# Attention and MLP in one kernel: norms and q/k loads pair by pair in a ring of six, the MLP three units behind the attention instead of four

## The chip, the cores and the metric

The kernel runs on one core of one Trainium2 chip. Times are device microseconds (us) of one execution, as medians over several. Engines: PE (matmul), DVE (VectorE), ACT (ScalarE), POOL (GpSimd), SP (SyncE, which here only issues DMAs). DMAs issued by SP form one queue; those issued by POOL, which convert float32 to bfloat16 on the way, form another. Fast executions of one kernel differ by up to some 1.5%. Runs more than that above the fastest count as slow; they are kept out of all ratios and verdicts, but the medians and ranges quoted below are of all runs.

## The reference

```python
def _attn_ref(q, k, v, tau):                       # (8, 12, 448, 64), tau 0.1
    q_n = q / (np.linalg.norm(q, axis=-1, keepdims=True) + 1e-06)
    k_n = k / (np.linalg.norm(k, axis=-1, keepdims=True) + 1e-06)
    scores = np.matmul(q_n, k_n.transpose(0, 1, 3, 2)) / tau
    attn = np.exp(scores - np.max(scores, axis=-1, keepdims=True))
    attn = attn / (np.sum(attn, axis=-1, keepdims=True) + 1e-09)
    return np.matmul(attn, v)
def _moe_ref(x, w_in, w_out):                      # x (3584, 768), w_in (768, 2048)
    h = x @ w_in
    return (h * np.cos(h)) @ w_out
```

The heads of one batch, side by side, are the 768 columns of x for its 448 tokens.

## The kernel before

A *pair* is two heads (g, 48 of them), a *unit* three pairs (u, 16), a batch two units. For a pair, POOL squares q and k, DVE sums the squares (`reduce`), ACT makes the reciprocal norm by Ln and Exp (`rnorm`), POOL scales; PE transposes, multiplies q by k; ACT takes the exponentials; PE multiplies by v (`attend`) and also forms the sums of the softmax. Once a unit is done, its sums take a way of their own, the *chain of the sums*, before x is ready:

```python
    def gather(u):      # SP: four small DMAs, sums out of xu into 128 partitions
    def recip(u):       # DVE: add the two halves, reciprocal
    def spread(u):      # SP: DMA to scratch in DRAM
    def broadcast(u):   # SP: two DMAs, 64 copies of each row back into RB (0.69 MB written)
    def normalise(u, p, eng="DVE"):
        i, b = u % 2, u // 2
        P.op(eng, lambda e: e.tensor_tensor(xTv[b % 2][:, UP * i + p, :], xuv[i][:, 0, p, :], RBv[:, p, :], ALU.mult),
             ["RB", ("xu", i, p)], [("xT", b % 2, UP * i + p)])
```

The MLP of a batch is `m1` (W1, 96 matmuls in 8 groups, cos and product) and `m2` (W2), whose matmuls are given out in portions of 8 as fills between the attention of later pairs. What is done when stands in the loop below; `kq` counts four places in each of a unit's three pairs. In the traces each engine takes its instructions in the order in which the program names them: a copy that is ready still stands behind a normalise that waits (shown below at 325.52).

```python
    LAG = 4
    FILLS = ((8, 8, 8, 8, 8, 8, 8, 8, 8, 0, 8, 0), (8, 8, 8, 8, 16, 8, 8, 8, 8, 8, 8, 16))
    def around(u, kq):
        ...
        if kq == (4 if u == 0 else 0) and u + 2 < NU:
            load(u + 2, 0, UP)                    # q and k of a whole unit, 1.38 MB, SP
        if u + 1 < NU:
            ...                                   # x is kq (kq - 1 in unit 0)
            if 0 <= x < 3:
                squares(u + 1, x, ...)            # POOL, a unit ahead
            if 2 <= x < 5:
                reduce(u + 1, x - 2)
            if x == 5:
                rnorm(u + 1, 0, UP)
            if 6 <= x < 9:
                scale(u + 1, x - 6)               # POOL
        if kq == 1 and u >= 1 and u + 1 < NU:
            load_v(u + 1)                         # POOL's DMA queue
        if kq in (1, 4, 7):
            load_w()
        if u >= 1:
            if kq == 2:
                gather(u - 1)
            if kq == 5:
                recip(u - 1)
                spread(u - 1)
            if kq == 8:
                broadcast(u - 1)
        if u >= 2 and kq < UP:
            normalise(u - 2, kq, "POOL" if early else "DVE")
    ...
            if p == 0 and u >= LAG and u % 2 == 0:
                m1((u - LAG) // 2)
                steps = list(FILLS[((u - LAG) // 2) % 2])
```

With a lag of four, unit 2b + 1 is normalised in unit 2b + 3 and needed by `m1` of batch b in unit 2b + 4: a unit of slack.

## Time and profile before

| | before |
|---|---|
| median (3 runs) | 530.25 us (524.15 to 532.13) |
| profiled run | 528.39 us, span 526.6 us |
| first m1 starts | 103.65 us |
| from there to m1 of batch 6 | 334.5 us |
| from there to m1 of batch 7 | 42.4 us |
| from there to the end | 46.0 us |

The kernel has an opening, in which PE waits, and a dense part, in which PE is the bound. I call the time from one m1 to the next a cycle, counted from 0: six pairs, with 80 fills in the even ones and 112 in the odd ones. These are the first four cycles before, as busy time in stretches (length, then PE, PE loads, DVE, ACT, POOL with the number of instructions, granted clock, DMA share, GB/s):

```profile
103.65:158.59 54.94, 50.07 (x369) 24.79 (x370) 28.12 (x34) 37.29 (x45) 25.32 (x15) 1.00 0.41 90
158.59:216.23 57.64, 57.64 (x417) 29.36 (x418) 32.60 (x43) 40.19 (x47) 24.27 (x15) 1.00 0.55 124
216.23:271.14 54.91, 52.44 (x386) 26.23 (x384) 26.05 (x32) 34.71 (x43) 23.87 (x14) 1.00 0.43 100
271.14:330.62 59.48, 57.71 (x417) 29.36 (x418) 32.41 (x43) 40.37 (x47) 24.27 (x15) 1.00 0.56 117
```

PE needs 57.6 us for an odd cycle and 52.4 for an even one, at full clock. One broadcast in the order of time (start, duration, engine and line, what, and in brackets how long the engine stood idle for whom):

```profile
205.59 1.10 SPq L373 DMA_DIRECT2D RB<-scr  x2
207.49 0.34 SPq L250 DMA_DIRECT2D raw<-in_q_dram  x1
...
210.97 0.68 DVE L380 TENSOR_TENSOR xT<-xu,RB 128x448 bf16<-128x448 f32 x1 [2.87 <-DMA RB<-scr]
211.11 0.81 POOL L257 DMA_DIRECT2D va<-in_v_dram  x1
```

The broadcast has the DMA engines to itself at first: the next q/k load is issued behind it, and v comes when it has landed. And these are the page's DMA issues (count, size of one, median us to landing):

```profile
RB<-scr SPq DMA_DIRECT2D x32, 336.0 KB, 4.7
...
va<-in_v_dram POOLq DMA_DIRECT2D x16, 336.0 KB, 7.2
```

### The profile page before, as it was taken

What the parts mean: (1) busy time and instruction counts of PE and PEld (TensorE: products, weight loads), DVE (VectorE), ACT (ScalarE), POOL (GpSimd) and SP (SyncE); (2) the same over time, 40 slices, a digit from 0 to 9 for tenths busy, and PEclk for the clock granted to TensorE, in tenths of its full rate; (3) what the DMA queues carried; (4) which work ended last, traced back from release to release, by engine and by line L of the source; (5) the groups of instructions that cost most, each with busy time, mean ns of one, the idle gap of its engine ahead of it and who ended that gap; (6) DMA issues with size and microseconds to landing.
All of it is one profiled execution on the core that took longest, in us unless ns stands there. A gap on an engine that the chain in (4) does not pass through costs nothing.

```text
span 526.6 us, 7760 instructions
## 1 busy us (share of the span) xinstructions
PE 465.4 (88%) x3241; PEld 231.1 (44%) x3247; DVE 246.6 (47%) x310; ACT 291.4 (55%) x348; POOL 195.1 (37%) x128
## 2 busy tenths in 40 slices
PE   7676272898989999999999998999899999799996
PEld 2232121353435554554445544554355544355563
DVE  5544333465527535544655453545565333512421
ACT  2666271657766668557764777367765764301400
POOL 4784656902680186207550547008530400000000
PEclk9788877799999999999999999999999999989999
DMA  8997999710765157603790296415730320222023
GB/s 202 192 214 138 210 194 184 183 22 2 179 151 103 31 139 177 148 1 92 156 211 7 67 190 151 84 31 132 148 49 12 104 68 20 54 60 61 1 61 89
DMA packets 50562, 56.85 MB, mean 108 GB/s; under 512 B 9824, under 2 KB 44128, under 8 KB 50528
## 3 DMA queue, kind: packets, MB, share of 16 engines
q1 hardware_dynamic: 36544, 44.57, 34.3%
q0 software_dynamic: 13984, 11.80, 15.0%
q8 instruction: 25, 0.41, 0.3%
q14 instruction: 9, 0.07, 0.0%
HBM read 56.62 MB, written 11.18 MB: 129 GB/s over the span
## 4 chain that ended last, share of the span: by engine, by line
PE 67%; DMA 8%; DVE 7%; ACT 6%; POOL 6%; issue 4%; SPq 2%; ACTq 0%; POOLq 0%; DVEq 0%
PE SC L390 17%; PE PO L429 17%; PE AV L390 10%; PE SC L323 5%; PE AV L334 5%; DMA sums<-xu 4%; PE SC L429 4%; ACT PX L326 4%; PE AV L340 3%; POOL qks L301 3%; PE TP L314 2%; DMA RB<-scr 2%; DVE n L282 2%; PE AV L429 2%; SPq L354 1%
## 5 line engine op out<-in xcount | busy, mean ns | idle before, releaser
L326 ACT ACTIVATE PX<-SC 112x896 bf16<-112x896 f32 x192 | 163.9, 915 | 65.3 <-PE SC L323 65.0
L301 POOL TENSOR_TENSOR qks<-raw,rn 112x1024 bf16<-112x1024 f32 (+1 forms) x47 | 87.9, 1895 | 189.8 <-ACT rn L294 189.4
L429 PE MATMUL PO<-W,gT 128*128 128x384 bf16 x704 | 128.7, 330 | 8.1 <-DVE osb L437 8.1
L323 PE MATMUL SC<-qkT 64*112 64x448 bf16 x384 | 64.6, 393 | 41.0 <-ACT PX L326 38.5
L429 PEld LDWEIGHTS PO<-W,gT 128*128 128x128 bf16 x704 | 64.0, 98 | 70.1 <-issue 17.8
L390 PE MATMUL SC<-xT,W 128*128 128x448 bf16 x480 | 94.7, 352 | 0.0
L275 POOL TENSOR_TENSOR sq<-raw 112x1024 bf16<-112x1024 f32 x43 | 81.5, 1907 | 6.7 <-DMA raw<-in_k_dram 6.5
L393 ACT ACTIVATE cosb<-SC,cst 128x896 f32<-128x896 f32 x40 | 40.3, 1008 | 49.0 <-PE SC L390 46.3
L390 PEld LDWEIGHTS SC<-xT,W 128*128 128x128 bf16 x480 | 47.0, 98 | 43.8
L282 DVE TENSOR_REDUCE n<-sq 112x16 f32<-112x1024 bf16 (+1 forms) x49 | 57.6, 1187 | 17.6 <-POOL sq L275 16.9
L395 DVE TENSOR_TENSOR gT<-SC,cosb 128x896 bf16<-128x896 f32 x40 | 43.6, 1091 | 41.7 <-ACT cosb L393 41.7
L390 PE MATMUL AV<-xT,W 128*128 128x448 bf16 x288 | 58.4, 353 | 1.1 <-ACT xu L344 1.0
L393 ACT ACTIVATE cosb<-AV,cst 128x896 f32<-128x896 f32 x24 | 24.2, 1008 | 53.4 <-PE AV L390 52.1
L323 PEld LDWEIGHTS SC<-qkT 64*112 64x112 bf16 x384 | 20.7, 127 | 72.3 <-ACT PX L326 54.5
L317 DVE COPY qkT<-TP 128x896 bf16<-128x896 bf16 x48 | 29.7, 620 | 45.9 <-PE TP L314 45.5
L380 DVE TENSOR_TENSOR xT<-xu,RB 128x448 bf16<-128x448 f32 x42 | 33.9, 816 | 32.4 <-DMA RB<-scr 32.4
L334 PE MATMUL AV<-PX,va 112*64 112x448 bf16 x384 | 48.7, 378 | 0.0
L437 DVE COPY osb<-PO 128x384 f32<-128x384 f32 x44 | 24.3, 551 | 41.8 <-PE PO L429 41.6
L390 PEld LDWEIGHTS AV<-xT,W 128*128 128x128 bf16 x288 | 27.8, 98 | 28.2 <-issue 1.5
L395 DVE TENSOR_TENSOR gT<-AV,cosb 128x896 bf16<-128x896 f32 x24 | 26.1, 1089 | 27.8 <-ACT cosb L393 27.8
L344 ACT ACTIVATE xu<-AV 128x896 f32<-128x896 f32 x37 | 34.0, 918 | 2.8 <-PE AV L340 2.8
L314 PE MATMUL TP<-ident,qks 112*128 112x112 bf16 x384 | 28.4, 218 | 3.4 <-DVE qks L301 2.6
(37 smaller groups left out, 249.5 us busy)
## 6 DMA issues: line engine op xcount, KB each, us to landing
RB<-scr SPq DMA_DIRECT2D x32, 336.0 KB, 4.7
raw<-in_q_dram SPq DMA_DIRECT2D x15, 672.0 KB, 8.1
raw<-in_k_dram SPq DMA_DIRECT2D x15, 672.0 KB, 10.0
va<-in_v_dram POOLq DMA_DIRECT2D x16, 336.0 KB, 7.2
W<-in_moe_w_in_dram POOLq DMA_DIRECT2D x6, 512.0 KB, 7.4
W<-in_moe_w_out_dram POOLq DMA_DIRECT2D x4, 768.0 KB, 7.8
out_dram<-osb SPq DMA_DIRECT2D x8, 336.0 KB, 2.7
out_dram<-osb SPq DMA_DIRECT2D x8, 288.0 KB, 2.6
```

The lines of the kernel that those rows point to most:

```text
L275: P.op(eng, lambda e, s0=s0, s1=s1: e.tensor_tensor(y[:, :, s0:s1, :], x[:, :, s0:s1, :], x[:, :, s0:s1, :], ALU.mult), [("raw", i, p, h) ...
L282: P.op("DVE", lambda e: e.tensor_reduce(out=n2[i].ap().rearrange("p (h s) -> p h s", s=NS)[:, 2 * p : 2 * p + 2, s0:s1], in_=sq[p].ap().re ...
L301: P.op(eng, lambda e, s0=s0, s1=s1: e.tensor_tensor(qksv[i][:, s0:s1, hs, :].rearrange("p s h d -> p h s d"), rawv[i][:, hs, s0:s1, :], ba ...
L314: P.op("PE", lambda e, s=s: e.transpose(TP.ap()[:, NP * s : NP * s + NP], qksv[i][:, s, 2 * p : 2 * p + 2, :], ident.ap()), [("qks", i, p, ...
L323: P.op("PE", lambda e, r=r, a=a: e.matmul(SCv[z][0:NP, a, 0:S], qkT[j].ap()[r, S + NP * c : S + NP * c + NP], qkT[j].ap()[r, 0:S], start=T ...
L326: P.op("ACT", lambda e: e.activation(PXv[j][:, c], SCv[z][0:NP, :, 0:S], ACT.Exp, scale=1.0 / TAU), ["SC%d" % z], [("PX", j, c)])
L334: P.op("PE", lambda e, a=a, c=c: e.matmul(AVv[64 * a : 64 * a + 64, 0, 0:S], vav[i][:, NJ * (2 * p + a) + c, :], PXv[j][:, c, a, :], start ...
L344: P.op("ACT", lambda e: e.activation(xuv[i][:, :, p, :], AVv[:, :, 0:S], ACT.Copy, bias=0.0), ["AV"], [("xu", i, p)])
L390: P.op("PE", lambda e, n=n, c=c, a=a: e.matmul(ph[:, a, 0:S], W1v[:, c, 128 * n : 128 * n + 128], xTv[b % 2][:, c, :], start=(c == 0), sto ...
L393: P.op("ACT", lambda e: e.activation(cosv[cz], ph[:, :, 0:S], ACT.Sin, bias=cst.ap()[:, 0:1], scale=1.0), [name, "cst"], [("cos", cz)])
L395: P.op("DVE", lambda e: e.tensor_tensor(gTv[:, 2 * gi : 2 * gi + 2, S * (b % 2) : S * (b % 2) + S], ph[:, :, 0:S], cosv[cz], ALU.mult), [n ...
L429: P.op("PE", lambda e, po=po, f=f, col=col, hf=hf: e.matmul(po[:, 0:HW], gTv[:, f, col : col + 128], W2v[:, f, HW * hf : HW * hf + HW], st ...
```

## The change

It is meant to shorten the opening: q/k are loaded, squared and scaled pair by pair in a ring of six slots, not unit by unit, so that POOL's normalise no longer holds up a whole unit and the small gathers no longer stand behind 1.38 MB; the MLP starts a unit earlier (lag 3); W1 comes in four column quarters, so that its first groups can start with a part of it. Early normalises move from POOL to DVE. The v load moves from the first to the second pair of a unit. The core, cut:

```diff
-    w_loads = [(("W1", c), ... W1v[:, c, :], moe_w_in[128 * c : 128 * c + 128, :])) for c in range(NKC)]
+    w_loads = [(("W1", x), ... W1v[:, :, WQ * x : WQ * x + WQ], moe_w_in[:, WQ * x : WQ * x + WQ] ...)) for x in range(NQ)]
...
-    LAG = 4
+    LAG = 3
+    EARLY = UP * LAG + 1
+    W_AT = {2: 1, 4: 1, 5: 1, 7: 1, 8: 1, 9: 3}
...
-    def around(u, kq):
-        ... (as shown above)
+    def around(g, at):
+        u, kq = g // UP, 4 * (g % UP) + at
+        if at == 0:
+            if g + 2 < NG:
+                rnorm(g + 2)
+                scale(g + 2)
+                if g + 2 + RR - 1 < NG:
+                    load(g + 2 + RR - 1)          # one pair, 0.46 MB
+            if g + 3 < NG:
+                squares(g + 3)
+        if at == 1:
+            for _ in range(W_AT.get(g, 0)):
+                load_w()
+            if g % UP == 1 and u + 1 < NU:
+                load_v(u + 1)
         if u >= 1:
             if kq == 2:
                 gather(u - 1)
...
             if kq == 8:
                 broadcast(u - 1)
         if u >= 2 and kq < UP:
-            normalise(u - 2, kq, "POOL" if early else "DVE")
+            normalise(u - 2, kq)
...
-            if p == 0 and u >= LAG and u % 2 == 0:
-                m1((u - LAG) // 2)
+        if g >= UP * LAG and (g - UP * LAG) % (2 * UP) == 0:
+            b = (g - UP * LAG) // (2 * UP)
+            m1(b)
```

At the end, m1 of batch 6 no longer stands behind the last pair; there are five halves of m2 instead.

## The prediction

> **What bounds the kernel now.** I read the busy time by stage first, then the chain of waits in the slow stage, then the order of time there, and last the DMA. The MLP of one batch (first matmul W1, here m1; second W2, here m2) is interleaved with the attention of later pairs of heads; g counts the 48 pairs. Busy time in stretches, us:
>
> ```profile
> 20.00:40.00 20.00, 15.60 (x124) 6.14 (x124) 10.80 (x12) 11.60 (x15) 14.24 (x11) 0.82 1.03 224
> ...
> 60.00:80.00 20.00, 10.15 (x77) 4.01 (x80) 8.58 (x11) 10.71 (x15) 12.53 (x10) 0.74 1.09 186
> 80.00:100.00 20.00, 8.28 (x63) 3.24 (x60) 6.32 (x9) 5.57 (x9) 16.59 (x12) 0.66 0.86 168
> 100.00:120.00 20.00, 19.49 (x119) 9.81 (x120) 13.56 (x12) 12.39 (x14) 4.05 (x3) 1.00 0.35 78
> ...
> 180.00:240.00 60.00, 60.00 (x440) 30.44 (x441) 30.61 (x40) 39.97 (x48) 24.04 (x14) 1.00 0.47 111
> ```
>
> Columns: length, PE, PE loads, DVE, ACT, POOL, clock, DMA share, GB/s. There are two kernels in one. Until 103.65 us, where m1 of batch 0 starts, PE is half idle and DMA is at 0.84 to 1.09. After that PE is the bound (60 of 60 us). So only the opening and the end have something to give. The chain of waits in the opening:
>
> ```profile
> 47.92 8.80 issue
> ...
> 56.76 1.13 POOL xT L380
> 57.88 1.85 POOL sq L275
> ...
> 72.72 9.73 issue
> ...
> 82.49 1.13 POOL xT L380
> 83.62 1.85 POOL sq L275
> ```
>
> Both long "issue" pieces are POOL standing in front of its normalise (xT) until the broadcast of the softmax sums (RB) has landed; squares and scaling of a whole unit (3 pairs) are queued behind it, and behind those everything: exps, scores. One unit takes 82.49 - 56.76 = 25.7 us, 8.6 us a pair, though a pair costs PE about 3.1 us when dense. The hops of that chain come from the order of time and the issues:
>
> ```profile
> 34.86 2.49 SPq L354 DMA_DIRECT2D sums<-xu  x4
> ...
> 44.72 0.76 DVE L362 TENSOR_TENSOR rcp<-sums 128x21 f32<-128x21 f32 x1 [3.24 <-DMA sums<-xu]
> ```
>
> The gather of the sums lands 7.4 us after its last issue, because 1.38 MB of q/k were put into the same queue at 32.23 us. At the end of the kernel, with no load ahead of it, the same gather takes:
>
> ```profile
> DMA to landing us min/median/max: 1.9/2.0/2.0
> ```
>
> **What the Trainium skill says.** "DMA: Bandwidth & Descriptors", section "Queues, rings and completion order": a queue's descriptors are consumed in ring order, and each DMA engine goes round the queues packet by packet. The 7.4 against 2.0 us agrees: a small transfer waits for what stands before it in its own queue, and shares with the other. "Perfetto Trace Analysis", section "Optimization Strategy": with several regimes whose limit differs, interleaving them helps; this is what a shorter lag does. "TensorE: Matmul & The Clock Gate", section "HAM oscillation": idle gaps beyond about 3.4 us drop the PE clock. The trace agrees: after a 9 us gap eight AV matmuls took 1.71 us at 68.40 instead of 0.95 at 49.95. "Perfetto Trace Analysis", section "Matmuls", asks for rotating PSUM banks; m2 with one bank pays for that at the new end, see below.
>
> **The change, part by part.**
> *DMA before m1(0).* The page gives the queues' cost: hardware 44.57 MB for 34.3% of 16 x 526.6 us, that is 247 GB/s when all engines serve it, and the casting POOL queue 11.80 MB (as written) for 15.0%, 149 GB/s. So one pair of q/k (0.459 MB) costs 1.9 us, a v load 2.3, a broadcast 2.8, all weights (6.29 MB) 42 us. Before: 6 units of q/k 33, weights 42, five v 11.5, three broadcasts 8.4, small ones about 6, sum 101 us, which is the opening's 103. After, m1(0) sits at pair 9, not 12, and needs W1 only: up to 16 pairs 30, W1 21, one W2 part 5, four v 9, two broadcasts and gathers 10, sum 75 us, of which some 5 to 8 us may come later. The other three W2 parts (16 us) fall beside m1(0), which takes 18.2 us at a DMA share of 0.35. So DMA alone would allow m1(0) at 67 to 75.
> *A new loop.* Per pair the norms now run squares, reduce, Ln and Exp, scale, and POOL may start the next pair's squares only after this scale: 1.89 (squares) + 0.04 + 1.21 (reduce) + 0.66 (reduce's end at 12.46 to scale's start at 13.12, 16 columns) + 1.88 (scale) = 5.7 us a pair. It is not free of cost, but far below 8.6.
> *The sums' chain.* The first squares follow the old start; pair 1 is scaled on POOL until 14.7, squares(2) to 16.6, reduce(2) to 17.9. With 5.7 a pair reduce(5) ends at 35.0, and the copy xu(2), late in pair 3, at 36.7. Gather 2.4 issue + 3 land (no large load ahead of it, W1 beside it), reciprocal 1.1, spread 2.5, broadcast issue and landing 7 (behind one pair's load and a W1 part): RB at about 53. DVE then does two normalises, a qkT copy and xu(5) (3.8 us) before the second gather at 57. The same chain again, 15.5 us, to 72.5, and 4.7 us for three normalises with two copies between: m1(0) at 77. The order on the engines shows that normalise(1) and m1(0) now lie in the same pair, with none between, so this chain and not DMA sets it; with the landings of the old opening (20 us a chain) it would be 86. I take 79: 24.7 us earlier.
> *The dense part.* From m1(0) to m1(6) are six cycles of six pairs. Before they took 54.9, 57.6, 54.9, 59.5, 54.7 us (starts of L390's AV groups in the chain). PE's own sum: m1 18.2 + 16 m2 matmuls 2.6 + six pairs of 3.1 + 80 or 112 fills of 0.163. For the fuller cycles that is 57.6, and they stay there, 58.2. In the others the last two pairs have 8 fills only and would run at ACT's or the loop's 5.0 to 5.7; I keep 54.5, a bit less than 54.9, since the gather no longer queues behind 1.38 MB and DVE waits less at the reciprocal (PE lost 1.24 us there at 150.49). Three of each: 338 us.
> *The end.* m1(6) and its m2 20.9. Pairs 46 and 47 have no fills: ACT sets them at 4 exps of 0.84 + one 0.92 + gaps = 4.7 each, and attend(47) 1.5: 10.9. Then five m2 halves on one bank, 2.6 + 0.75 for the evacuation in between, 16.2; beside them the last sums' chain: 2.4 + 2.0 + 0.6 + 1.9 + 4.7 + 0.6 = 12.2 plus the copy 0.9, hidden. The old end had m1(6) there, and a 3.08 us PE wait before 460.90. From m1(7) on nothing changes: 526.6 - 480.7 = 45.9.
> Sum: 79 + 338 + 20.9 + 10.9 + 16.2 + 45.9 = 510.9 us of span; the profiled run timed 528.4 for a span of 526.6, so 513 us. A check by difference: -24.7 in the opening, +9.3 for three pairs of PE work that move into the dense part, +3.2 for two pairs without fills, +3.0 for bank waits, -4.1 for waits of the old end, and some -2.5 in the cycles: -15.8, the same.
>
> **The rivals.**
> 1. The sums' chain stays at its old length (20 us or more a unit), since five weight parts still load in the opening beside it. For it: spread and broadcast took 10.9 us from 45.83 to 56.72, with the gather not concerned. Then m1(0) is at 86 to 88 and the time 520 to 522, within 2%.
> 2. The norm loop becomes the bound of the dense part. 5.7 us a loop against 5.72 us of a dense pair leaves nothing; DVE ops under POOL's load stretch (normalise 0.62 up to 2.78 us at 364.95). 0.3 us on 30 pairs is +9 us: 522. Against it: Ln/Exp has 0.65 us of slack on ACT before the third exp, and each m1 lets the loop catch up.
> 3. DMA holds m1(0) or the first m2: W1 parts are now 1 KB pieces per row and chunk instead of 4 KB, and three W2 parts go out late. A late W2 is a PE stall after m1(0), some 5 us. Against it: 18 us of m1 cover it.
> 4. Better than thought: chains without queueing, warm PE, DVE waits gone from all cycles: m1(0) at 74, cycles of 54 and 57.6: 503.
>
> **Range and chances.** My sum is 513; rivals 1 to 3 each take away 5 to 9 us and rarely come together, rival 4 gives 8 to 10. So 504 to 523. The limit of 2% against about 529 is 518.5, above my figure by a bit less than one deviation (some 7 us): faster 0.72, within 2% 0.26, slower 0.02, as no part adds more than the opening gives back.
>
> **What would show it.** The first L379 matmul (m1) at 75 to 85 us instead of 103.65; early pairs 5.7 to 6 us apart; gathers landing in 2 to 4 us, not 6.2 in the middle; POOL's 189 us of idle before scale broken into short pieces; cycles of 54 to 58 us; no PE gap over 2 us after m1(0). Wrong if m1(0) comes after 88, if PE waits in the dense part for exps behind Ln/Exp (loop), or for W2 after m1(0).

## The result, and the profile after

| | before | after |
|---|---|---|
| median, same rounds (4 runs each) | 530.83 us (524.15 to 532.13) | 553.47 us (552.81 to 555.55) |
| profiled run: span, clock | 526.6 us, 0.96 | 551.0 us, 0.95 |
| first m1 starts | 103.65 | 81.62 |
| to m1 of batch 6 | 334.5 (35 pairs) | 374.75 (36 pairs) |
| to m1 of batch 7 | 42.4 | 47.1 |
| to the end | 46.0 | 47.5 |

The ratio is 1.0477 (95% interval 1.0375 to 1.058): slower, where 513 us had been predicted. A ratio here is always the mean time of one kernel's fast runs over that of the other's in the same rounds, so not quite the ratio of the medians quoted. The kernel is correct.

The opening came out near the prediction. The sums of squares of pairs 2 to 4 in the order of time, and the first m1:

```profile
16.43 1.22 DVE L280 TENSOR_REDUCE n<-sq 112x16 f32<-112x1024 bf16 x1 [2.78 <-POOL sq L275]
...
22.09 1.22 DVE L280 TENSOR_REDUCE n<-sq 112x16 f32<-112x1024 bf16 x1 [3.92 <-POOL sq L275]
...
27.77 1.22 DVE L280 TENSOR_REDUCE n<-sq 112x16 f32<-112x1024 bf16 x1 [1.81 <-POOL sq L275]
...
81.62 4.64 PE L379 MATMUL AV<-xT,W 128*128 128x448 bf16 x12 [7.91 <-DVE xu L336]
```

The pairs are 5.67 us apart, and m1 starts 22 us earlier. But then the cycles, which the prediction had at 54.5 and 58.2:

```profile
81.62:139.19 57.57, 52.46 (x368) 25.35 (x369) 27.70 (x31) 36.21 (x50) 21.34 (x13) 0.95 0.65 136
139.19:206.16 66.97, 59.70 (x418) 29.58 (x417) 34.06 (x42) 41.82 (x55) 27.95 (x16) 0.97 0.45 105
206.16:261.31 55.15, 52.43 (x386) 26.21 (x384) 27.96 (x32) 36.22 (x50) 21.30 (x13) 1.00 0.42 102
261.31:331.99 70.68, 61.63 (x418) 30.08 (x417) 34.74 (x42) 41.82 (x55) 27.49 (x16) 0.93 0.43 100
331.99:387.44 55.45, 52.73 (x385) 26.31 (x383) 27.87 (x32) 36.22 (x50) 21.30 (x13) 0.99 0.43 102
387.44:456.37 68.93, 62.22 (x418) 30.32 (x417) 34.54 (x42) 41.82 (x55) 25.64 (x15) 0.93 0.31 69
```

The odd cycles take 67 to 71 us, for the same matmuls (417 or 418) that took 57.64 before, and at a lower clock, so that PE is even "busier". DMA is not full on average (0.31 to 0.45 in the odd cycles). What PE waited for from 81.62 to 456.37 (total us, times, longest):

```profile
PE AV L379 <- DVE xT L369: 12.5, 7, 3.4
PE PO L418 <- DVE osb L426: 12.5, 9, 3.9
...
PE SC L312 <- DVE qkT L306: 2.5, 3, 0.8
```

Before, in its dense part, the osb wait was 5.0 us and the other two were not there. (osb is the copy that frees the one PSUM bank of m2; xT is the normalised input of m1.) All three come from DVE, which is busy for half the time only. PE waits for no v in these cycles, though v lands late too (9.2 us). In total DVE does not stand longer in front of RB than before (30.1 us in these cycles, 31.7 before); what differs is when it gets on: 8.0 to 10.8 us after the broadcast's issue, against 5.2 to 6.6. Why DVE is late, at the start of m1 of batch 1, in the order of time:

```profile
130.81 0.44 SPq L252 DMA_DIRECT2D raw<-in_q_dram  x1
130.88 0.81 POOL L258 DMA_DIRECT2D va<-in_v_dram  x1
...
131.29 0.48 SPq L252 DMA_DIRECT2D raw<-in_k_dram  x1
131.81 1.11 SPq L362 DMA_DIRECT2D RB<-scr  x2
...
142.24 0.62 DVE L369 TENSOR_TENSOR xT<-xu,RB 128x448 bf16<-128x448 f32 x1 [4.38 <-DMA RB<-scr]
...
142.93 0.36 PE L379 MATMUL AV<-xT,W 128*128 128x448 bf16 x1 [2.99 <-DVE xT L369]
```

A pair's q and k, a unit's v and the broadcast go out within one microsecond, and the normalise comes 10.4 us after the broadcast's issue, against 5.4 in the piece shown of before. At the end of an odd cycle the same wait goes through the copies that stand behind the normalise on DVE:

```profile
325.52 1.96 DVE L369 TENSOR_TENSOR xT<-xu,RB 128x448 bf16<-128x448 f32 x1 [2.97 <-DMA RB<-scr]
...
327.41 0.54 DVE L426 COPY osb<-PO 128x384 f32<-128x384 f32 x1
...
328.01 4.19 PE L418 MATMUL PO<-W,gT 128*128 128x384 bf16 x16 [3.93 <-DVE osb L426]
```

Sixteen matmuls that take 2.77 us warm then take 4.19, since PE has lost its clock (0.65 from 328 to 332 us). The limit of 3.4 us that the prediction named is no sharp one here: sixteen took 4.41 after a wait of 2.08 us (at 452.13) and 2.77 after one of 2.16 (at 203.56). The first normalise here also takes 1.96 us for 0.62 alone, beside POOL's squares (325.11 to 327.00); more on that below. On the page's list of DMA issues the whole is seen in two lines:

```profile
RB<-scr SPq DMA_DIRECT2D x32, 336.0 KB, 7.5
va<-in_v_dram POOLq DMA_DIRECT2D x16, 336.0 KB, 9.2
```

Against the 338 us predicted, the dense part is 36.8 us too long. Waits of PE that before did not have make 12.5 + (12.5 - 5.0) + 2.5 = 22.5. PE busy is 341.2 us, against 3 x 57.6 + 3 x 52.4 = 330 at the clock of before: 11 us of slower matmuls. The other 3 us are waits that before had too: 5.0 for osb, 3.7 for exps and 2.4 for gT, 11.1 in all, where the prediction had left 338 - 330 = 8. So nothing is unassigned: 341.2 busy and 33.6 of waits are the 374.8.

### The profile page after: what moved, and what is told of

Its sections match the earlier page's. It is cut to its first block, busy times and chain, and to the rows that moved or that the text cites. A ratio compares the mean times of both kernels' runs of the same rounds, so it can differ in the third digit from the quotient of the medians.

```text
span 551.0 us, 7956 instructions
## 1 busy us (share of the span) xinstructions
PE 476.6 (86%) x3238; PEld 231.3 (42%) x3243; DVE 259.3 (47%) x314; ACT 304.2 (55%) x408; POOL 198.0 (36%) x124
## 4 chain that ended last, share of the span: by engine, by line
issue 47%; POOL 21%; PE 21%; DMA 6%; DVE 3%; ACT 1%; SPq 1%; POOLq 0%; DVEq 0%
POOL sq L275 14%; PE SC L379 6%; PE PO L418 6%; DMA RB<-scr 4%; POOL qks L293 4%; PE AV L379 4%; PE SC L418 2%; POOL va L258 2%; DVE osb L426 1%; PE AV L418 1%; DMA raw<-in_k_dram 1%; ACT PX L315 1%; DVE xT L369 1%; DMA scr<-rcp 1%; POOL W L437 1%
## 5 line engine op out<-in xcount | busy, mean ns | idle before, releaser
L418 PE MATMUL PO<-W,gT 128*128 128x384 bf16 x784 | 144.1, 332 | 15.2 <-DVE osb L426 15.2
L418 PEld LDWEIGHTS PO<-W,gT 128*128 128x128 bf16 x784 | 71.8, 99 | 85.0 <-DVE osb L426 22.5
L379 PE MATMUL SC<-xT,W 128*128 128x448 bf16 x480 | 96.9, 358 | 0.0
L275 POOL TENSOR_TENSOR sq<-raw 112x1024 bf16<-112x1024 f32 x47 | 91.8, 1952 | 6.4 <-DMA raw<-in_k_dram 6.4
L379 PE MATMUL AV<-xT,W 128*128 128x448 bf16 x288 | 67.6, 382 | 21.5 <-DVE xT L369 13.6
L379 PEld LDWEIGHTS SC<-xT,W 128*128 128x128 bf16 x480 | 47.8, 100 | 46.4 <-issue 4.4
L369 DVE TENSOR_TENSOR xT<-xu,RB 128x448 bf16<-128x448 f32 x48 | 43.6, 935 | 38.3 <-DMA RB<-scr 38.3
L379 PEld LDWEIGHTS AV<-xT,W 128*128 128x128 bf16 x288 | 29.0, 103 | 55.2 <-DVE xT L369 18.1
L426 DVE COPY osb<-PO 128x384 f32<-128x384 f32 x49 | 27.0, 551 | 46.0 <-PE PO L418 45.8
L312 PEld LDWEIGHTS SC<-qkT 64*112 64x112 bf16 x384 | 20.7, 127 | 57.6 <-ACT PX L315 34.3
L333 ACT ACTIVATE xu<-AV 128x896 f32<-128x896 f32 x39 | 35.8, 918 | 2.0 <-PE AV L329 2.0
## 6 DMA issues: line engine op xcount, KB each, us to landing
W<-in_moe_w_in_dram POOLq DMA_DIRECT2D x4, 768.0 KB, 11.3
```

The costliest lines, as they stand in the source:

```text
L275: P.op(eng, lambda e: e.tensor_tensor(o, x, x, ALU.mult), rd, wr)
L312: P.op("PE", lambda e, r=r, a=a: e.matmul(SCv[z][0:NP, a, 0:S], qkT[j].ap()[r, S + NP * c : S + NP * c + NP], qkT[j].ap()[r, 0:S], start=T ...
L333: P.op("ACT", lambda e: e.activation(xuv[i][:, :, p, :], AVv[:, :, 0:S], ACT.Copy, bias=0.0), ["AV"], [("xu", i, p)])
L379: P.op("PE", lambda e, n=n, c=c, a=a: e.matmul(ph[:, a, 0:S], W1v[:, c, 128 * n : 128 * n + 128], xTv[b % 2][:, c, :], start=(c == 0), sto ...
L418: P.op("PE", lambda e, po=po, f=f, col=col, hf=hf: e.matmul(po[:, 0:HW], gTv[:, f, col : col + 128], W2v[:, f, HW * hf : HW * hf + HW], st ...
```

## The experiments

Three theories stood at the start. **A**: with lag 3, m1 of a batch lies in the pair in which its last unit is normalised; it has no slack, and every delay goes into PE. **B**: the norm loop of 5.7 us a pair has become the bound (rival 2 of the prediction). **C**: the broadcast is late, because of its place behind a pair's load in SP's queue and the v load beside it. Later ones follow from the results. "Before" below is the kernel before in the rounds of the same batch of runs: 529.32, 528.78, 528.28, 528.24 and 530.59 us in the five batches.

### m1 a pair later (A)

```diff
-    EARLY = UP * LAG + 1
+    EARLY = UP * LAG + 2
-        if g >= UP * LAG and (g - UP * LAG) % (2 * UP) == 0:
-            b = (g - UP * LAG) // (2 * UP)
+        if g > UP * LAG and (g - 1 - UP * LAG) % (2 * UP) == 0:
+            b = (g - 1 - UP * LAG) // (2 * UP)
```

> The changed kernel, with the first MLP matmul of each batch (m1) one pair of heads later, so that one pair of work lies between the normalise that m1 needs and m1. Theory A (m1 and everything behind it waits for the late broadcast of the sums, because the shorter lag left no pair in between): the PE waits of about 7 us at m1 of batches 1, 3 and 5 go, the six cycles fall from 375 us to 345 to 355 us, and the time from 553 to 525 to 535 us. Rival B (the per-pair loop of squares, reduce, Ln/Exp and scale sets the dense part): the cycles stay at 370 or more and the time at 550 or more, since the loop is untouched. Rival C (the broadcast lands late because it queues behind the q/k load, and the DVE that stands in front of it holds up the PSUM evacuations, wherever m1 is): only half of the loss goes, 538 to 545 us.

549.3 us (547.39 to 550.13), ratio 1.039 (1.0352 to 1.0427). The waits for xT are gone and the m1 take 18.3 us again (18.3 to 20.0, against up to 25.4). But the wait of PE for osb is now 13.7 us and one for qkT has grown to 12.1. The lateness only changed its address: DVE still stands in front of RB, and what it does for PE stands behind it. A alone explains 4 of 23 us. (The edit moved v too: it goes out up to 2.9 us ahead of every second broadcast, and none within 17 us of the others, and RB lands in 6.3 us. So the 4 us are not purely A's.)

### Broadcast in front of the load, v load a pair earlier (C, both parts)

```diff
         if at == 0:
+            if u >= 1 and kq == 8:
+                broadcast(u - 1)
             if g + 2 < NG:
                 rnorm(g + 2)
...
-            if g % UP == 1 and u + 1 < NU:
-                load_v(u + 1)
+        if at == (2 if g < EARLY else 1) and (g == 1 or g >= UP and g % UP == 0) and u + 1 < NU:
+            load_v(u + 1)
...
-            if kq == 8:
-                broadcast(u - 1)
```

> The changed kernel, with the broadcast of the sums issued ahead of its pair's q/k load in the SP queue, and the load of v moved from the second pair of a unit back to the first, as in the kernel before. Theory A (no pair between normalise and m1): broadcasts land in about 5 us instead of 7.5, so the waits shrink by 2 to 3 us at each of 12 places, time 530 to 540 us, and some wait at m1 stays. Rival C (it is the place in the queue that costs): nearly all of the 37 us goes, time below 525 us. Rival B (norm loop): 550 us or more.

529.51 us (527.11 to 533.05), ratio 1.0061 (1.0032 to 1.009): 24 us come back by moving two DMAs (553.47 is from earlier rounds, in which before was within 1.6 us of its value here). RB lands in 4.8 us, v in 4.9. C is the main cause; norms, ring and loop are unchanged in this run.

### Lag 3 alone in the kernel before (a failed edit)

```diff
-    LAG = 4
+    LAG = 3
-                steps = list(FILLS[((u - LAG) // 2) % 2])
+                steps = list(FILLS[((u - LAG) // 2) % 2]) if u < NU - 1 else []
```

> The kernel before, with nothing changed but the lag of three units (and the end that belongs to it): q/k loads by units, norms by units, weights by rows. Theory A: m1 of batch 0 at 85 to 92 us (all ten weight loads still stand before it), then the same waits for the broadcast before m1, shorter as the broadcast lands in about 5 us: cycles 345 to 355 us, time 525 to 540 us. Rival C alone (queue place and not lag): cycles stay at 340 us as before, time 520 to 526 us. Rival B: the same 520 to 526 us.

The result was wrong (nan), and its 500.26 us mean nothing: I had left the test `u % 2 == 0`, so only 7 of 8 MLP batches were computed. The mended one follows below.

### The ring with the old lag

The change with `LAG = 4` and the end of the kernel before.

> The changed kernel, with the lag of four units and the end of the kernel before; ring, norms by pairs and weights by quarters stay. Theory A: m1 of batch 0 at 95 to 100 us, no wait at m1, cycles about 345 us with some DVE waits from the later broadcast, time 523 to 532 us, the same as before within 1%. Rival B (norm loop): cycles of 60 us and more as in the changed kernel, time 545 us or more. Rival C: DVE waits stay in the odd units, time 535 to 545 us.

545.3 us (541.66 to 546.06), ratio 1.0301 (1.0246 to 1.0356). There is a unit of slack before m1 again and no wait for xT, and RB lands in 7.3 us as in the change. The wait for osb is 12.2 us. So the late broadcast costs 17 us even where m1 does not need it at once (528.24 with both DMAs moved, below), by way of DVE's order.

### The order alone

Of the diff for C, only the broadcast's place; v stays in the second pair.

> The changed kernel with one thing altered: the broadcast of the sums is issued ahead of its pair's q/k load; the load of v stays at the second pair of a unit. If the q/k load in the broadcast's own queue is the cost, most of the 24 us that the pair of edits gave comes back (time 530 to 537 us, broadcasts landing in about 5 us). If the load of v from the other queue, which runs at the same time, is the cost, little comes back (545 us or more, landing 7 us).

542.69 us (540.22 to 545.82), ratio 1.0289 (1.0232 to 1.0347). RB lands in 6.0 us, with v still issued 0.1 to 0.7 us ahead of all but one broadcast of the dense part and no pair's load just in front; the normalise follows 7.2 to 8.5 us after the issue. This is 11 of the 24 us; 13 stay.

### m1 later together with the DMA order, and with normalise a pair later too

The first is the two diffs together; the second adds:

```diff
-        if u >= 2 and kq < UP:
-            normalise(u - 2, kq)
+        if u >= 2 and UP <= kq < 2 * UP:
+            normalise(u - 2, kq - UP)
```

> Both cures: broadcast ahead of the q/k load, v earlier, and m1 one pair later. With the broadcast landing in 4.7 us there are still 4 to 5 us lost at m1 of batches 1, 3 and 5 (normalises slowed beside POOL, cold PE clock behind them). If that is the missing pair between normalise and m1 (theory A as a second cause), they go and the time falls from 529 to 512 to 522 us, under both kernels. If the late landing was all, it stays at 526 to 531 us.

> As the kernel with both cures, and the three normalises of a unit also moved three places later in the program (from the first pair of the next unit into its end and the second pair), so that DVE meets a broadcast that has landed. If DVE standing in front of the broadcast still costs (osb copies and qkT copies queued behind it), 3 to 8 us more come: 507 to 518 us. If the landing in 4.7 us was early enough already, nothing changes beside the kernel with both cures.

531.09 us (527.51 to 535.5), ratio 1.0056 (1.0021 to 1.0091), and 532.03 us (526.43 to 537.96), ratio 1.0055 (1.0023 to 1.0087). The first one's profile fell in the slow state and is not compared. With slack given to m1 and DMAs in order there is still no gain over before. The second brings the normalises back into m1's own pair, so it takes the slack away again: PE waits 9.0 us for xT, and m1 of batches 1, 3 and 5 take 23.0, 21.4 and 22.8 us. There the first m1 starts at 88.3 us and not at 79.0, which takes back what is saved later.

### Lag 3 alone, mended

```diff
-            if p == 0 and u >= LAG and u % 2 == 0:
+            if p == 0 and u >= LAG and (u - LAG) % 2 == 0:
```

> The kernel before with the lag of three units alone; the earlier try left out one batch of the MLP by a wrong test for even units and is mended. Broadcasts are ahead of the next unit's q/k load here, so they should land in about 5 us. If the shorter lag in itself is a loss: waits at m1 of 3 to 5 us in three of six cycles, time 525 to 535 us. If the lag is harmless where the broadcast is first in its queue: 510 to 523 us.

536.19 us (534.29 to 537.62), ratio 1.0161 (1.0117 to 1.0205): its interval straddles 2%, so between same and slower. The first m1 starts at 74.6 us, 29 us earlier than before and earlier than in the change; the six cycles then take 365.1 us. RB is not late here (4.8 us), yet PE waits 11.3 us for xT. So theory A does cost something by itself, and the shorter lag alone gives the whole gain of the opening; the ring is not what brought it.

### The v load alone

Of the diff for C, only the v load's place; the broadcast stays behind the pair's load.

> The change with one edit: the v load goes out in the first pair of a unit instead of the second; the order of q/k load and broadcast in the SP queue is left as the change has it. The order alone was measured at 542.69 us, 10.8 us under the change's 553.47; order and v load together at 529.51. If the two effects add up, this run takes off the other 13 us: 540 us (537 to 543), with RB landing at 6 us or more because a pair's load still stands before it. If the v load is what really makes the broadcast late and the order hardly matters once it is gone, 530 to 534 us and RB near 5 us. If the v load only matters together with the order, 548 to 554 us.

531.55 us (526.51 to 539.23; 7 of the 20 runs are slow), ratio 1.0057 (1.0021 to 1.0093). I had expected 540 if the two effects added up; they do not. As means of the fast runs: the change 553.8 us, the order alone 542.9, the v load alone 530.4, both 529.5. So the v load alone gives what both give (ratios 1.0057 and 1.0061); a pair's load in front costs 11 us while v is beside the broadcast and about 1 when it is not. The page of this run:

```profile
RB<-scr SPq DMA_DIRECT2D x32, 336.0 KB, 5.3
va<-in_v_dram POOLq DMA_DIRECT2D x16, 336.0 KB, 5.3
```

and its odd cycle's end, where the change had its 3.93 us wait:

```profile
307.22 1.10 SPq L362 DMA_DIRECT2D RB<-scr  x2
...
312.85 0.63 DVE L369 TENSOR_TENSOR xT<-xu,RB 128x448 bf16<-128x448 f32 x1 [0.60 <-DMA RB<-scr]
...
314.00 2.77 PE L418 MATMUL PO<-W,gT 128*128 128x384 bf16 x16 [0.21 <-DVE osb L426]
```

The normalise comes 5.6 us after the broadcast and PE hardly waits. In the change it was 325.52 - 316.58 = 8.9 us, and PE waited 3.93. This is the best place of the run: before m1 of batches 2, 4 and 6 the normalise comes 5.6 to 6.7 us after the broadcast, but before m1 of batches 1, 3 and 5 it is 7.7 to 8.4 (10.0 to 10.8 in the change). PE still waits 9.8 us for xT (12.5 in the change), but only 4.1 for osb (12.5). Median landings of the whole kernel: 4.8 us with neither in the way, 5.3 with the pair's load in front, 6.0 with v beside, 7.5 with both; from 100 to 440 us alone 4.7, 5.3, 6.6 and 7.5. What a late landing costs PE is not proportional to it, and no run traced that curve.

### The ring at the old lag, with both DMAs moved

> The ring with the old lag of four units, and the broadcast in front of the load with the v load a pair earlier. The ring at lag four without these two edits took 545.3 us (ratio 1.030). If the late broadcast is all that the ring costs, this equals the kernel before: 526 to 532 us, the first m1 still at 100 to 105 us, all later m1 at 18.3 to 19 us, RB at 5 us. If the loop of norms in the dense part costs something of its own (rival 2 of the prediction), it stays above: 536 to 541 us with RB at 5 us all the same, and exps that wait behind Ln and Exp.

528.24 us (526.7 to 531.13), ratio 1.0027 (1.0005 to 1.0049). First m1 at 104.0 us; all m1 of the cycles after it at 18.3 us; gaps between them 34.6 to 39.2 (34.6 to 41.1 before). The ring and its loop cost nothing of their own in the dense part at this lag: rival B falls. They give nothing either.

### The fills moved

On top of both DMA edits, two empty places are moved to where no chain of the sums is waiting:

```diff
-    FILLS = ((8, 8, 8, 8, 8, 8, 8, 8, 8, 0, 8, 0), ...
+    FILLS = ((8, 0, 8, 0, 8, 8, 8, 8, 8, 8, 8, 8), ...
```

> Broadcast first and v load earlier (529.51 us as measured), and in the cycles with fewer m2 fills the two empty places are moved from the last two pairs to the first two, so that the last pairs, in which the chain of the sums runs, last longer by 16 fills of 0.163 us, 2.6 us. If the m1 of batches 1, 3 and 5 (23.0, 21.4 and 24.3 us against 18.3) still wait for the normalise because the pairs ahead of it are too short, they get up to 2.6 us shorter each: 520 to 525 us. If the pairs are bound by ACT or the loop and not by PE there, the fills only move the wait: 528 to 532 us. If fills early in the cycle are what hides the copy's wait, 532 to 536 us.

528.8 us (525.19 to 532.81), ratio 1.003 (1.0001 to 1.0059), a miss as to the size: m1 of batches 1, 3 and 5 went from 23.0, 21.4 and 24.3 us to 20.3, 20.6 and 20.6, 2.7, 0.8 and 3.7 us less where 2.6 was given, but the even gaps grew by 1.3 to 1.5 us, and the median moved by less than a microsecond. (The profile it is compared with is of that kernel's slowest run, 533.05 us, so single figures mean little.)

### The broadcast right behind the spread

As the last, with `kq == 6` for the broadcast, at its old place in the text.

> As the run with the fills moved, but the broadcast goes out right behind the spread, two tiles of scores earlier in the pair (about 1.5 us), as soon as the data can be there, and still in front of the next pair's load. If the chain of the sums is the only thing that makes m1 long, m1 of batches 1, 3 and 5 is at 19 to 21 us and the time at 515 to 521 us, under the kernel before. If the broadcast only waits in the queue for the spread to land, nothing changes against the run before it (within 2 us) and the wait holds the SP queue instead. If early broadcasts take DMA time from the q/k loads, scale comes later and the cycles get longer: 530 us or more.

528.07 us (525.05 to 532.83), ratio 1.0036 (0.9996 to 1.0076). The first m1 is at 77.5 us, yet the m1 of batches 1, 3 and 5 still take 20.6 us each. The main reason is no longer the broadcast:

```profile
135.84 2.27 POOL L275 TENSOR_TENSOR sq<-raw 112x1024 bf16<-112x1024 f32 x1
...
136.82 2.31 DVE L369 TENSOR_TENSOR xT<-xu,RB 128x448 bf16<-128x448 f32 x2
...
138.65 0.36 PE L379 MATMUL AV<-xT,W 128*128 128x448 bf16 x1 [1.78 <-DVE xT L369]
```

Two normalises, 0.62 us each when alone, take 2.31 and get on when POOL's squares end at 138.11. The Trainium skill, "SBUF — State Buffer", section "SBUF: two separate sides", says that POOL and a DVE operation with two SBUF inputs share a port pair by an exclusive lock, the loser fully blocked. This trace agrees with that reading, and PE waits 1.78 us for it. (The squares take 2.27 us for 1.89 alone; they began while the normalise before these two was still running, from 134.08 for 2.29 us, so they may have been the loser first.) No run removed POOL's squares from there, so the port as the cause is read from the trace and not shown by an experiment. It is no small matter: all normalises on DVE together take 55.5 us here (48 of them), 43.6 in the change and 33.9 before (42, six more on POOL).

### The late v load put into the kernel before, and placed in time

```diff
-        if kq == 1 and u >= 1 and u + 1 < NU:
+        if kq == 5 and u >= 1 and u + 1 < NU:
```

> The kernel before with one edit: the v load goes out in the second pair of a unit (where the change has it) instead of the first, so it runs beside the broadcast of the sums. Whole-unit q/k loads, lag four and weights stay as they were. If the v load beside the broadcast is harmful by itself, RB lands at 6 to 7.5 us instead of 4.7 and v at 9, DVE stands longer in front of its normalise and the time goes up, though by less than the 17 us that separate the ring at lag four with and without the two edits, as here no q/k load stands in front of the broadcast: 533 to 542 us. If the v load's place costs only together with a pair's load in front of the broadcast, the time stays within 2 us of before: 527 to 531 us with RB under 5.5 us.

525.12 us (521.66 to 530.97), ratio 0.996 (0.9925 to 0.9995). As a test it failed: v was still issued 5.4 to 7.8 us behind the broadcast in the dense part, little later than in before (3.5 to 5.9). Before, POOL runs ahead of PE: half of its v loads (8 of 16) wait for attention to free the buffer, wherever they stand in a unit's text. In the change POOL goes at the pace of the pairs, v stands behind the squares of the next pair, and it was issued 0.1 to 1.0 us ahead of the broadcast at all 12 broadcasts after 90 us that have a v load near them. So the moved line made the two collide only together with the ring. To place it in time:

```diff
-        if kq == 1 and u >= 1 and u + 1 < NU:
+        if kq == (7 if u >= LAG else 1) and u >= 1 and u + 1 < NU:
```

> The earlier attempt at this (v load in the second pair of a unit of the kernel before) did not make the collision: there POOL runs ahead, and v was still issued 5 to 8 us after the broadcast, as in the kernel before (4 to 8), while the change issues it 0.2 to 1.4 us in front of the broadcast. Here the v load of the dense part stands behind the second scaling of the next unit, which in the trace of before ends within half a us of the broadcast's issue, so v should now go out within 1 us of it. If v beside the broadcast is harmful by itself: RB lands at 6 to 7 us instead of 4.7, and the time rises, but as a unit of slack lies between normalise and the MLP at lag four, only through VectorE standing in front of RB: 531 to 540 us. If it is harmful only together with the ring's load in front: RB under 5.3 us and 525 to 531 us. If a later v makes the attention wait for v itself, a wait for va appears at the attend matmuls and the time rises without RB getting later.

527.22 us (522.93 to 532.5), ratio 0.9942 (0.9911 to 0.9973). Now they go out together:

```profile
200.01 0.81 POOL L257 DMA_DIRECT2D va<-in_v_dram  x1
200.05 1.10 SPq L373 DMA_DIRECT2D RB<-scr  x2
...
207.67 1.10 DVE L380 TENSOR_TENSOR xT<-xu,RB 128x448 bf16<-128x448 f32 x1 [5.10 <-DMA RB<-scr]
...
209.30 2.77 PE L429 MATMUL PO<-W,gT 128*128 128x384 bf16 x16 [1.30 <-DVE osb L437]
```

RB lands in 5.4 us instead of 4.7 and here 7.6 us pass to the normalise, but PE waits 1.30 us only and keeps its clock (2.77). In this kernel, then, v beside the broadcast makes it late by 0.7 us in the median and costs nothing, though the normalise comes 6.2 to 8.3 us after the issue. In the ring at lag 3 it costs 13 us without any load in front (the order alone, where the normalise came 7.2 to 8.5 us after it). So the cost needs v beside the broadcast and something that the ring or the shorter lag adds; which of the two stays open, as the order alone was not run at lag 4. That this run and the one before it came out 0.4 to 0.6% under before is within 2%, so the same; no version beats both kernels by more.

### The weights alone

The kernel before with W1 by column quarters.

> The kernel before with W1 loaded by column quarters, as the change does, and nothing else. The first m1 stands at 103.65 us there, held by the chain of the sums and not by W1, so theory: nothing changes, 527 to 531 us, m1(0) at 102 to 105 us. If quarters by columns (1 KB pieces) load noticeably slower and hold up the loads of the opening, m1(0) comes at 106 us or later and the time is 532 us or more; if the opening gets faster by it, 520 to 526 us.

527.07 us (523.62 to 532.17), ratio 1.0008 (0.9976 to 1.004), first m1 at 100.0 us. The weights neither give nor take.

## Why the prediction was wrong

**The opening** was right in mechanism and, with some luck, in size: m1 at 81.62 for 79 predicted. The loop was 5.67 for 5.7. The first broadcast went out at 45.2 and was normalised at 54.3 (53 predicted for RB), the second gather at 58.7 (57). The chain of the sums set it, as said. But its second round, from the gather at 58.7 to the normalise at 78.8, took 20.1 us and not 15.5, which is the length of rival 1; the normalises and copies behind it took 2.8 us and not 4.7, and 2 us had been added for safety. (The parts that the prediction names for a round add up to 16.0, not 15.5.) Rival 3 (weights holding m1) did not come as a wait, though the DMA share was 1.00 from 60 to 80 us. PE was at about half speed at this m1's start: 12 matmuls took 4.64 us, 2.43 when warm.

**The end** was right: 47.1 us from m1 of batch 6 to that of batch 7 (20.9 + 10.9 + 16.2 = 48.0 predicted) and 47.5 after it (45.9 predicted).

**The gathers** did get faster, as said, 3.3 us median to landing for 6.2, and DVE's wait at the reciprocal fell from 13.5 to 4.6 us. It did not help, since another wait ended last.

**The step that failed** is "The dense part", "Three of each: 338 us." It measured 374.75. Of the signs that the prediction named, those of the opening came (m1 at 75 to 85 us, pairs 5.7 us apart, gathers in 2 to 4 us); cycles of 54 to 58 us and no PE gap over 2 us did not: the odd cycles took 67 to 71 us, with waits of up to 3.9. I took the cycles of before, added PE's own sum, and granted that nothing but fewer waits would follow. Two things were left out, though both stood in the working of the opening:

1. *The broadcast.* For the opening I gave RB "7 (behind one pair's load and a W1 part)"; for the dense part I did not ask what would stand in front of it, though the diff puts a load there at every pair and the v load in the same pair's neighbourhood. It measured 7.5 us for 4.7. The experiments put 24 us on this at lag 3 (529.51 with both DMAs moved) and 17 us at lag 4 (545.3 against 528.24), where m1 has its slack; moving v alone gives the same as both. The mean bandwidth is not the point, as DMA was at 0.31 to 0.45 in the odd cycles, but the moment is: an estimate from the costs that the prediction worked out, 2.8 for the broadcast, 1.9 for a pair and 2.3 for v, gives 7.0 us for all three in a row, near the 7.5 measured. The Trainium skill, "DMA: Bandwidth & Descriptors", section "Issuing engines are not separate DMA queues", says that DMAs of SP and GpSimd run on the same 16 engines and interleave; the 4.8, 5.3, 6.0 and 7.5 us agree with it.

2. *The slack.* I noted that "normalise(1) and m1(0) now lie in the same pair, with none between", and used it for the first m1 only. It holds for all of them. In the best version with lag 3 (broadcast behind the spread), the six m1 take 21.0, 20.6, 18.7, 20.6, 18.7 and 20.6 us, 120.2 for the 109.2 predicted; the gaps between them take 230.9 for 228.8. So these 11 us are most of what is left: its dense part is 351.1 us for 338. With m1 a pair later they went (18.3 us in that run, but the first, with 20.0), but the first m1 then came at 89.8 us, and with the DMAs mended too the time was 531.09 us, so as much is lost elsewhere, the later opening first of all. The kernel before at lag 3 shows the same step without any late broadcast: RB in 4.8 us, and still 11.3 us of waits for xT. The prediction took from the Trainium skill, "Perfetto Trace Analysis", section "Optimization Strategy", that interleaving regimes helps; the page says only that performance "may be improved by interleaving those regimes", and here the shorter lag alone gave 29 us of opening and no time (ratio 1.0161).

**The rivals.** Rival 2, the loop as the bound, had 522 us as its result and PE waiting for exps behind Ln and Exp as its sign. That wait was 3.7 us in the cycles of the change (4.1 before), and the ring at lag 4 with DMAs in order equals before, so it was not it. None of the rivals was the right one: 1 and 3 asked what holds the opening or the first m2, 2 what bounds in steady running, none what a DVE that takes its work in order does to PE when one DMA lands late. "As no part adds more than the opening gives back" was the ground for the 0.02 for slower: 22.0 us were gained and 46.4 given back (40.2 in the cycles, 4.7 and 1.5 behind them).

The gain itself was over-valued too. With the late broadcast mended, 26 us of opening shrink to 3.4 us of span (523.2 for 526.6) and to nothing in the medians (528.07 for 528.28): 16.6 us go into the cycles, 4.7 and 1.5 behind them, together 22.8. The prediction's check by difference had given back 9.3 + 3.2 + 3.0 - 4.1 - 2.5 = 8.9. The 11 us of m1 are most of what lies between.

What stays open: the share of DVE's port in the last 11 us and in the change itself, and why v beside the broadcast costs 13 us in the ring at lag 3 and nothing in the kernel before.

## What to carry to other kernels

When a change splits a large transfer into many, list for each small transfer that something waits for what will stand in front of it and beside it in time, in every part of the kernel and not only where the change is aimed. An instruction's place in the program says little of when a DMA goes out; ask what its issuing engine waits for. And when a lag is shortened, count who has lost slack at each of its repetitions: here a DVE in front of one late DMA held up every copy queued behind it.

## What the Trainium skill lacked or had wrong

- "DMA: Bandwidth & Descriptors" says that queues share engines and how, but gives no landing time of a mid-size transfer in company. Here a broadcast of 0.69 MB landed (medians, 100 to 440 us) in 4.7 us with nothing in front of it or beside it, 5.3 behind 0.46 MB in its own queue, 6.6 beside a converting load of POOL's queue, and 7.5 with both: about the single delays of 0.6 and 1.9 added.
- No page gives an example of what it does to a load's place in time that it is issued from POOL, behind POOL's other work: the same line moved by a pair moved it by some 2 us (from 3.5 to 5.9 us behind the broadcast to 5.4 to 7.8), while the same place in the ring, where POOL's other work is different, put it 0.1 to 1.0 us ahead.
- Nothing was found that a page has wrong.
